# Converting the first two weight chunks by halves, and moving attention products next to scores

## The chip, the core and the metric

The kernel runs on one core of one Trainium2 chip. Its time is the device time of one launch in microseconds (us); the median of three runs of the kernel before is 542.89 us (542.35 to 542.96). TensorE (PE) multiplies matrices, VectorE (DVE), ScalarE (ACT) and GpSimd (POOL) work element by element, and SyncE (SP) issues most transfers. Each engine takes its own instructions in the order in which they stand in its queue.

## The reference

Inputs: `q`, `k`, `v` of shape (2, 8, 768, 64), weights of three layers, and two numbers, 8 global and 96 local positions. All arithmetic is float32.

```python
scores = q @ k.T / sqrt(64) - slope[h] * dist      # dist: to the key, or n_local for a global key
scores = where(keep, scores, -1e9)                  # keep: the 8 global keys, or the last 96 positions
a = exp(scores - max); a /= sum(a) + 1e-9
x = (a @ v) as (1536 tokens, 512)
h = x @ w_in                                        # 512 -> 2048
g = where(h > 0, h, exp(min(h, 0)) - 1)
x = g @ w_out                                       # 2048 -> 512
h = max(x @ w1, x @ w2, x @ w3)                     # 512 -> 768, three times
out = h @ w_out2                                    # 768 -> 512
```

## The kernel before, in words

Tokens are worked on in six groups of 256 (`GRP`), and three blocks of 512 (`BLOCKS`) for the first feed-forward layer. Attention is cut into 48 steps; step k is one tile of 128 queries for two heads. A step has these parts, each a method of `Windowed`: scores on PE (`scores_pe`, L214), a fused add and minimum on DVE (`scores_dve`, L239), exponentials with their sums on ACT (`scores_act`, `sums`), a reciprocal and a scaling on DVE (`recip`, `norm`), a transposition on PE (`turn_pe`, into a PSUM tile), its copy to SBUF (`turn_act`), and the product with the values on PE (`values_pe`, L318; `pair_pe` for two steps, `due_pe` for those that are due). The result is then copied (`pair_out`, `due_out`) or split at once into a high and a low part (`values_high`, `values_low`).

Steps 0 to 15 (the first block's tokens) run alone, in the loop of `windowed` at L1221. Steps 16 and 17 stand written out at L1250 to L1284, and steps 18 to 47 are laid beside the feed-forward layer in `Feed.run` (L765): one step to each column chunk `fc` (16 of them) of a block `bi`. For a chunk, `run` issues the product `h` of x with the chunk's `w_in` (12 matmuls, L674), then ELU on ACT and DVE (`elu_exp`, `elu_max`), the split of its result (`high` on ACT, `low` on DVE), and, one chunk late, the product `y` with the chunk's `w_out` (8 matmuls L705 and 4 matmuls L713). The same step's attention parts stand between these.

Weights come as 64-bit words and are converted on the chip before their first use, in the first block alone: a chunk is 128 x 2 x 512 (half 0 is `w_in`, half 1 `w_out`), and goes through `c_rebase` (ACT, L457), `c_low` (DVE, L461), two `c_word` (DVE, L468), `c_high` (ACT, L476) and `c_rest` (DVE, L481). Every one of these takes both halves in one instruction of 128 x 1024. In the loop of steps 0 to 15, a list of pieces, `words`, adds one piece of the conversion of chunks 0 and 1 to each step from step 8 (`CONV`) on. Chunk fc+1 is finished, and chunk fc+2 begun, beside chunk fc of the first block.

`FILL` (L43) adds two matmuls to the listed steps whose result nobody reads. The first four y tiles of a block are PSUM tiles that the block before has used; `save` (L721) copies them out first, half of it on ACT and half on DVE.

The order of the work is the order in which the code issues it; there is no scheduler.

## Time and profile before

| | |
|---|---|
| time of the runs, median | 542.89 us |
| the profiled execution's own time | 542.19 us |
| its span, first to last instruction | 540.4 us |
| PE busy | 530.7 us (98%) |
| DVE busy | 393.7 us (73%) |
| ACT busy | 288.0 us (53%) |
| chain that ended last | PE 91%, DVE 5%, ACT 3% |
| granted clock of PE, mean | 0.998 |

A span is the time from the first to the last instruction; the 1.8 us between it and the execution's time lie around it. Busy times of PE count each matmul to its modelled end, so neighbours overlap; what one matmul costs in a stream is the distance from its start to the next one's start. The busy shares are means over the whole span, and the stages differ: DVE is busy 90% or more in each fortieth of the span from 40.5 to 135 us, and 40% to 60% in most of those from 149 to 257 us. The rows that the prediction uses stand in a section of their own below.

### The profile page before, as it was taken

Reading aid. Unit: us, or ns where it says so; the run is one execution under the profiler, and the core shown is the slowest. Engines: PE = TensorE matmul, PEld = TensorE weight load, DVE = VectorE, ACT = ScalarE, POOL = GpSimd, SP = SyncE. Lnnn points to the kernel's source line nnn. Section 1 sums busy time; section 2 is a strip of 40 time slices with the busy share of each in tenths; the row PEclk is TensorE's granted clock in tenths of the full one; section 3 lists DMA queues with packets and bytes.
Section 4 is the critical chain, followed back from the end, with each engine's and each line's share of the span. In section 5 each row is a group of like instructions: output and inputs, shape, how many; then the busy total and the mean of one; then the engine's idle time right before and its main releaser. Section 6 shows DMA issues by size and latency. Waiting matters only on the chain.

```text
span 540.4 us, 7751 instructions
## 1 busy us (share of the span) xinstructions
PE 530.7 (98%) x2746; PEld 426.8 (79%) x2746; DVE 393.7 (73%) x828; ACT 288.0 (53%) x649; POOL 82.9 (15%) x89
## 2 busy tenths in 40 slices
PE   8999999999999999999999999999999999999995
PEld 6667787777777888888888888888888888888884
DVE  6889999999854444443567656787886989779883
ACT  5979877888845555554545655552157321224020
POOL 4220000000000000000000044321034410335000
PEclk9999999999999999999999999999999999999999
DMA  8929055442310111000000031331029301876014
GB/s 284 397 95 409 21 196 196 156 161 83 101 46 24 45 44 44 21 19 1 0 2 0 1 117 40 116 115 42 1 71 308 146 1 40 270 293 234 1 73 168
DMA packets 23455, 59.21 MB, mean 110 GB/s; under 512 B 2416, under 2 KB 2416, under 8 KB 23408
## 3 DMA queue, kind: packets, MB, share of 16 engines
q1 hardware_dynamic: 18368, 49.46, 26.5%
q10 hardware_dynamic: 5040, 9.18, 4.5%
q8 instruction: 24, 0.39, 0.3%
q14 instruction: 23, 0.19, 0.1%
HBM read 49.19 MB, written 9.44 MB: 108 GB/s over the span
## 4 chain that ended last, share of the span: by engine, by line
PE 91%; DVE 5%; ACT 3%; issue 0%; POOL 0%; ACTq 0%; POOLq 0%
PE h L674 26%; PE y L705 16%; PE y L713 8%; PE y L975 8%; PE y L1069 5%; PE y L674 5%; PE S L975 4%; PE TX L327 3%; PE TX L304 3%; PE S L228 3%; PE S L1069 2%; PE TX L975 2%; PE S L674 2%; PE h L975 2%; PE TX L1069 2%; ACT p L275 1%
## 5 line engine op out<-in xcount | busy, mean ns | idle before, releaser
L674 PE MATMUL h<-xh,w 128*128 128x512 f32 (+1 forms) x432 | 122.2, 387 | 0.2 <-ACT w L476 0.2
L705 PE MATMUL y<-gh,w 128*128 128x512 f32 x384 | 98.7, 399 | 0.1
L510 POOL TENSOR_TENSOR w<-wr,w 128x512 fp32r<-128x512 f32 x42 | 62.9, 1507 | 231.8 <-ACT w L509 220.5
L674 PEld LDWEIGHTS h<-xh,w 128*128 128x128 f32 x432 | 80.2, 188 | 17.9 <-ACT w L476 0.8
L705 PEld LDWEIGHTS y<-gh,w 128*128 128x128 f32 x384 | 69.7, 188 | 14.3 <-issue 0.5
L674 PE MATMUL h<-xl,w 128*128 128x512 f32 (+1 forms) x216 | 71.0, 386 | 0.0
L699 DVE SCALAR_TENSOR_TENSOR e<-e,h 128x512 f32<-128x512 f32 x48 | 32.9, 685 | 49.5 <-ACT e L695 49.4
L509 ACT CAST w<-wr 128x512 fp32r<-128x512 f32 x42 | 27.6, 663 | 63.4 <-DVE wr L500 51.1
L694 ACT ACTIVATE e<-h 128x512 f32<-128x512 f32 x48 | 28.7, 599 | 55.3 <-PE h L674 51.2
L275 ACT ACTIVATE p<-p,m 128x232 f32<-128x232 f32 (+1 forms) x96 | 44.9, 471 | 17.1 <-DVE m L254 16.9
L713 PE MATMUL y<-gl,w 128*128 128x512 f32 x192 | 51.6, 390 | 0.0
L500 DVE SCALAR_TENSOR_TENSOR wr<-wr 128x512 uint32<-128x512 uint32 x48 | 44.2, 921 | 7.5 <-ACT wr L492 6.0
L686 DVE TENSOR_TENSOR gl<-e,gh 128x512 fp32r<-128x512 f32 x48 | 33.1, 689 | 19.9 <-ACT gh L681 19.9
L674 PEld LDWEIGHTS h<-xl,w 128*128 128x128 f32 x216 | 40.4, 188 | 8.1 <-issue 0.2
L198 POOL TENSOR_SCALAR raw<-raw,qsc 128x256 f32<-128x256 f32 x24 | 16.8, 699 | 193.4 <-DMA raw<-qk 193.4
L975 PE MATMUL y<-t,w 128*128 128x512 f32 x180 | 42.7, 389 | 0.0
L713 PEld LDWEIGHTS y<-gl,w 128*128 128x128 f32 x192 | 36.0, 188 | 8.0 <-issue 0.3
L681 ACT CAST gh<-e 128x512 fp32r<-128x512 f32 x48 | 29.6, 616 | 23.5 <-DVE e L699 23.3
L468 DVE SCALAR_TENSOR_TENSOR wr<-wr 128x1024 uint32<-128x1024 uint32 (+1 forms) x36 | 39.8, 1120 | 0.4
L975 PEld LDWEIGHTS y<-t,w 128*128 128x128 f32 x180 | 33.8, 188 | 7.0
L695 ACT ACTIVATE e<-e 128x512 f32<-128x512 f32 x48 | 30.3, 632 | 1.5
L985 ACT CAST g<-m 128x512 fp32r<-128x512 f32 x18 | 10.9, 621 | 35.2 <-DVE m L1004 27.0
(155 smaller groups left out, 837.5 us busy)
## 6 DMA issues: line engine op xcount, KB each, us to landing
wr<-wa SPq DMA_DIRECT2D x14, 1024.0 KB, 6.9
wr<-wb SPq DMA_DIRECT2D x24, 512.0 KB, 4.6
v<-v SPq DMA_DIRECT2D x24, 256.0 KB, 2.8
part<-row ACTq DMA_DIRECT2D x24, 256.0 KB, 4.6
raw<-qk SPq DMA_DIRECT2D x16, 312.0 KB, 4.6
row<-part SPq DMA_DIRECT2D x12, 256.0 KB, 3.1
out<-rows ACTq DMA_DIRECT2D x11, 256.0 KB, 2.3
raw<-qk SPq DMA_DIRECT2D x8, 260.0 KB, 4.7
```

The source lines that it names most:

```text
L275: self.nc.scalar.activation(p[:, o], p[:, o], AF.Exp, bias=m[:, u:u + 1], scale=-1.0, accum_out=m[:, 2 + u:3 + u],)
L468: self.nc.vector.scalar_tensor_tensor(r[..., 0], r[..., 1], v, r[..., 0], op0=op, op1=ALU.bitwise_or)
L500: self.nc.vector.scalar_tensor_tensor(t, a, c, t, op0=op, op1=ALU.bitwise_or)
L510: nc.gpsimd.tensor_tensor(w[:, u, 1], v, w[:, u, 0].bitcast(F32), op=ALU.subtract)
L674: nc.tensor.matmul(out[:, o:n], w[:, part % 2, c * P:c * P + P], (xl if part == 2 else xh)[:, c, o:n], start=(c, part) == order[0], stop=( ...
L686: (engine or self.nc.vector).tensor_tensor(gl[:, 0:n], e[:, 0:n], gh[:, 0:n].bitcast(F32), op=ALU.subtract)
L695: self.nc.scalar.activation(e, e, AF.Exp, scale=-1.0)
L699: self.nc.vector.scalar_tensor_tensor(e, e, -1.0, h, op0=ALU.add, op1=ALU.max)
L705: self.nc.tensor.matmul(y[e][:, 0:n], w[:, a, e * P:e * P + P], g[0][:, 0:n], start=fc == 0 and a == 0, stop=False,)
L713: self.nc.tensor.matmul(y[e][:, 0:n], w[:, 0, e * P:e * P + P], g[1][:, 0:n], start=False, stop=fc == NFC - 1,)
L975: self.nc.tensor.matmul(out, w[:, u, i % 2, b + c * P:b + c * P + P], o[:, i // 2, c], start=c == i == 0, stop=c == 1 and i == 2,)
L1069: nc.tensor.matmul(o, t[:, a, r], w[:, u, b], start=u == k == 0, stop=u == 1 and k == 2,)
```

## The change

Chunks 0 and 1 are converted by halves (the methods take `h`), half 0 in the loop of steps 8 to 15, half 1 later. Steps 18 and 19, with the chunks fc = 0 and 1 of the first block, leave `run` and stand in a new method, `begin`, in an order of their own; `run` starts at fc = 2 there. The filling matmuls of steps 8 to 13 go. At the first two chunks of the second block (steps 34 and 35) the value products are now those that are due (`joint = bi < 2`), and stand ahead of the scores.

```diff
-FILL = {1: 2, 2: 2, 8: 2, 9: 2, 10: 2, 11: 2, 12: 2, 13: 2}
+FILL = {1: 2, 2: 2}
...
-    def parts(self, c):
+    def parts(self, c, h=None):
+        hs = slice(0, 2) if h is None else slice(h, h + 1)
         if c in self.whole:
-            return [(self.whole[c], slice(0, 2))]
+            return [(self.whole[c][:, hs], hs)]
...
+    def begin(self, at, k, x, h):
+        copy, n = self.nc.scalar.copy, BLOCKS[0]
+        w = self.w[1][:, 0]
+        at.load_values(k)
+        self.w_ahead(4)
+        at.scores_pe(k, m=2)
+        at.turn_pe(k - 2, "y2")
+        h1 = self.ps.tile([P, 512], F32, tag="y3", name="h1")
+        self.product(h1, w, x, n, 0, 0, 4, BEHIND)
+        at.recip(k - 1)
+        at.norm(k - 1)
+        self.c_low(1, 1)
+        at.turn_pe(k - 1)
+        self.product(h1, w, x, n, 0, 4, 8, BEHIND)
+        e = self.elu_exp(h, n)
+        at.turn_act(k - 2, copy)
+        at.turn_act(k - 1, copy)
+        self.elu_max(e, h)
+        at.scores_dve(k)
+        gh = self.high(e, n)
+        gl = self.low(e, gh, n)
+        prev = gh, gl
+        self.c_high(0, 1)
+        self.c_rebase(2)
+        self.c_low(2)
+        self.c_rest(0, 1)
+        self.c_word(2, 0)
+        at.pair_pe(k - 2)
+        e = self.elu_exp(h1, n)
+        self.elu_max(e, h1)
+        at.scores_act(k)
+        at.sums(k)
+        at.pair_out(k - 2, copy)
+        y = self.out_tiles()
+        self.out_high(y, 0, prev, n)
+        self.out_low(y, 0, prev, n)
+        self.c_word(2, 1)
+        at.recip(k)
+        at.norm(k)
+        self.c_high(2)
+        k += 1
+        at.turn_pe(k - 1)
+        at.turn_act(k - 1, copy)
...
+        self.c_rest(2)
+        at.scores_dve(k)
+        at.scores_act(k)
+        at.sums(k)
+        gh = self.high(e, n)
+        self.c_word(1, 0, 1)
+        self.c_word(1, 1, 1)
+        self.c_high(1, 1)
+        self.c_rebase(3)
+        at.recip(k)
+        at.norm(k)
+        gl = self.low(e, gh, n)
+        self.c_rest(1, 1)
+        self.c_low(3)
+        self.c_word(3, 0)
+        return y, (gh, gl)
...
-                joint = fc > 1
+                joint = bi < 2
...
+                late = bi == 0 or fc > 0
+                if not late:
+                    at.due_out(due, nc.vector.tensor_copy)
+                    if joint:
+                        at.turn_pe(k - 1)
                 if left:
                     self.out_low(*left)
-                late = bi == 0 or fc > 0
                 if not late:
                     at.turn_act(k - 1, nc.vector.tensor_copy)
-                    if k % 2 == 0:
-                        at.pair_pe(k - 2)
                     at.scores_dve(k)
                     e = self.elu_exp(h, n)
                     at.scores_act(k)
-                    if k % 2 == 0:
-                        at.pair_out(k - 2, nc.scalar.copy)
...
         def convert():
-            f.c_rebase(0)
-            f.c_low(0)
+            f.c_rebase(0, 0)
+            f.c_low(0, 0)
             yield
-            f.c_word(0, 0)
-            f.c_rebase(1)
+            f.c_word(0, 0, 0)
+            f.c_rebase(1, 0)
             yield
-            f.c_word(0, 1)
+            f.c_word(0, 1, 0)
+            f.c_low(1, 0)
             yield
-            f.c_high(0)
-            f.c_low(1)
+            f.c_high(0, 0)
+            f.c_word(1, 0, 0)
             yield
-            f.c_rest(0)
+            f.c_rest(0, 0)
+            f.c_rebase(0, 1)
             yield
-            f.c_word(1, 0)
+            f.c_word(1, 1, 0)
+            yield
+            f.c_high(1, 0)
+            f.c_low(0, 1)
+            yield
+            f.c_rest(1, 0)
             yield
...
         at.values_low(k - 4, x)
+        f.c_word(0, 0, 1)
         at.scores_pe(k, m=2)
...
         at.values_high(k - 2, x)
+        f.c_rebase(1, 1)
         at.scores_act(k)
         at.scores_dve(k + 1, True)
         at.values_low(k - 2, x)
+        f.c_word(0, 1, 1)
         at.values_pe(k - 1)
...
-        f.run(at, first + 2, x, h, lambda: covered(nc, at.const, ni, flag))
+        begun = f.begin(at, k + 2, x, h)
+        f.run(at, first + 4, x, begun, lambda: covered(nc, at.const, ni, flag))
```

DVE, from the reciprocal of step 17 on, before: `wr_283` is chunk 1 as loaded, `wr_401` chunk 2, `w_712` chunk 1 converted, `m` the sums of a step, `p` its probabilities, `e` the ELU.

```order
L266 RECIPROCAL m_651<-m_651 128x2
L288 TENSOR_SCALAR p_650<-p_650,m_651 128x232 x2
L468 SCALAR_TENSOR_TENSOR wr_283<-wr_283 128x1024
L699 SCALAR_TENSOR_TENSOR e_702<-e_702,h_145 128x512
L254 ISA p_708,m_709<-S0_695,rel_105 128x232
L254 ISA m_709 128x1
L254 ISA p_708,m_709<-S1_696,rel_105 128x232
L254 ISA m_709 128x1
L461 TENSOR_SCALAR wr_401<-wr_401 128x1024
L481 TENSOR_TENSOR w_712<-wr_283,w_712 128x2x512
L266 RECIPROCAL m_709<-m_709 128x2
L288 TENSOR_SCALAR p_708<-p_708,m_709 128x232 x2
```

DVE behind the scores of step 18 (`p_716`) in the changed kernel: `wr_395` is now chunk 2, `w_456` and `w_766` are chunks 0 and 2 converted, `h1_688` is the product of fc = 1, and `p_778` belongs to step 19.

```order
L689 TENSOR_TENSOR gl_722<-e_710,gh_720 128x512
L462 TENSOR_SCALAR wr_395<-wr_395 128x1024
L482 TENSOR_TENSOR w_456<-wr_205,w_456 128x512
L469 SCALAR_TENSOR_TENSOR wr_395<-wr_395 128x1024
L702 SCALAR_TENSOR_TENSOR e_737<-e_737,h1_688 128x512
L469 SCALAR_TENSOR_TENSOR wr_395<-wr_395 128x1024
L266 RECIPROCAL m_717<-m_717 128x2
L288 TENSOR_SCALAR p_716<-p_716,m_717 128x232 x2
L482 TENSOR_TENSOR w_766<-wr_395,w_766 128x2x512
L254 ISA p_778,m_779<-S0_677,rel_105 128x232
L254 ISA m_779 128x1
L254 ISA p_778,m_779<-S1_678,rel_105 128x232
```

Chunk 1 is whole ahead of chunk 2's words before; now its second half comes behind the scores of step 19, and the low part of chunk 2 stands ahead of those scores.

PE behind the first product of the second block, before: `p_1659` and `p_1712` are steps 32 and 33, `S0_1790` and `S1_1791` the scores of steps 34 and 35, `y` the last chunk of the first block.

```order
L304 MATMUL TX_1785<-ident_126,p_1712 116x128 x4
L228 MATMUL S0_1790<-raw_1604 128x232
L228 MATMUL S1_1791<-raw_1604 128x232
L228 MATMUL S0_1790<-raw_1604 128x232
L228 MATMUL S1_1791<-raw_1604 128x232
L713 MATMUL y_787<-gl_1733,w_1663 128x512
L713 MATMUL y_788<-gl_1733,w_1663 128x512
L713 MATMUL y_789<-gl_1733,w_1663 128x512
L713 MATMUL y_790<-gl_1733,w_1663 128x512
L327 MATMUL TX_1785<-p_1659,v_1633 64x128 x4
L327 MATMUL TX_1785<-p_1712,v_1633 64x128 x4
```

The same place now: `p_1653` is step 32 and `p_1706` step 33.

```order
L327 MATMUL TX_1779<-p_1653,v_1627 64x128 x4
L228 MATMUL S0_1784<-raw_1598 128x232
L228 MATMUL S1_1785<-raw_1598 128x232
L228 MATMUL S0_1784<-raw_1598 128x232
L228 MATMUL S1_1785<-raw_1598 128x232
L304 MATMUL TX_1792<-ident_126,p_1706 116x128 x4
L716 MATMUL y_746<-gl_1727,w_1657 128x512
L716 MATMUL y_747<-gl_1727,w_1657 128x512
L716 MATMUL y_748<-gl_1727,w_1657 128x512
L716 MATMUL y_749<-gl_1727,w_1657 128x512
```

The transposition of step 33 has moved from ahead of the scores to behind them, the value product of step 32 to the head, and that of step 33 to the next even step.

## Rows read from the trace of the kernel before

**Rows 1.** Busy time by stretch: PE, PEld, DVE, ACT, POOL; clock; DMA share, GB/s

```profile
13.50:27.00 13.50, 12.89 (x111) 8.71 (x111) 12.09 (x53) 12.82 (x48) 3.10 (x5) 1.00 1.03 396
```

**Rows 2.** Chain of waits, attention's end: start us, us, what

```profile
51.93 1.13 ACT w L476
```

**Rows 3.** PE's timeline, first block: start us, us, instruction, count, idle before and releaser

```profile
53.10 0.50 PE L674 MATMUL h<-xh,w 128*128 128x512 f32 x1 [0.21 <-ACT w L476]
...
57.71 0.65 PE L304 MATMUL TX<-ident,p 128*116 128x128 f32 x4
...
66.87 0.40 PE L674 MATMUL h<-xh,w 128*128 128x512 f32 x1
```

**Rows 4.** DVE's timeline, steps 8 to 23

```profile
18.18 0.40 DVE L254 CUSTOM_DVE_ANT_0 p<-S,rel 128x232 f32<-128x232 f32 x1 [0.34 <-PE S L228]
...
20.55 0.39 DVE L254 CUSTOM_DVE_ANT_0 p<-y,rel 128x232 f32<-128x232 f32 x1
...
22.09 1.22 DVE L468 SCALAR_TENSOR_TENSOR wr<-wr 128x1024 uint32<-128x1024 uint32 x1
...
39.38 0.40 DVE L254 CUSTOM_DVE_ANT_0 p<-S,rel 128x232 f32<-128x232 f32 x1 [0.69 <-PE S L228]
...
43.25 0.17 DVE L266 RECIPROCAL m<-m 128x2 f32<-128x2 f32 x1 [0.29 <-ACT m L237]
...
52.36 0.39 DVE L254 CUSTOM_DVE_ANT_0 p<-S,rel 128x232 f32<-128x232 f32 x1
...
56.07 2.48 DVE L468 SCALAR_TENSOR_TENSOR wr<-wr 128x1024 uint32<-128x1024 uint32 x2
...
79.21 0.69 DVE L699 SCALAR_TENSOR_TENSOR e<-e,h 128x512 f32<-128x512 f32 x1 [0.44 <-ACT e L695]
```

**Rows 5.** DVE's timeline: conversion of late chunks, which comes by halves already

```profile
134.82 0.76 DVE L461 TENSOR_SCALAR wr<-wr 128x512 uint32<-128x512 uint32 x2
...
138.00 2.49 DVE L468 SCALAR_TENSOR_TENSOR wr<-wr 128x512 uint32<-128x512 uint32 x4
```

**Rows 6.** ACT's timeline, first block

```profile
40.73 0.49 ACT L275 ACTIVATE p<-p,m 128x232 f32<-128x232 f32 x1
...
52.96 0.49 ACT L275 ACTIVATE p<-p,m 128x232 f32<-128x232 f32 x1
...
56.24 0.60 ACT L694 ACTIVATE e<-h 128x512 f32<-128x512 f32 x1 [0.41 <-PE h L674]
...
57.41 0.25 ACT L390 COPY xraw<-TX 128x128 f32<-128x128 f32 x1
...
65.50 1.13 ACT L476 CAST w<-wr 128x1024 fp32r<-128x1024 f32 x1
```

**Rows 7.** PE's timeline, start of the second block

```profile
154.27 0.60 PE L304 MATMUL TX<-ident,p 128*116 128x128 f32 x4
154.80 1.05 PE L228 MATMUL S<-raw 64*128 64x232 f32 x8
...
156.90 1.09 PE L327 MATMUL TX<-p,v 116*64 116x128 f32 x16
...
161.16 2.08 PE L705 MATMUL y<-gh,w 128*128 128x512 f32 x8
```

**Rows 8.** DVE's timeline there

```profile
154.91 0.69 DVE L315 COPY p<-TX 116x512 f32<-116x512 f32 x1 [1.96 <-PE TX L304]
...
159.07 0.17 DVE L266 RECIPROCAL m<-m 128x2 f32<-128x2 f32 x1 [1.86 <-ACT m L237]
159.27 0.59 DVE L288 TENSOR_SCALAR p<-p,m 128x232 f32<-128x232 f32 x2
159.78 1.41 DVE L727 COPY yraw<-y 128x256 f32<-128x256 f32 x4
```

**Rows 9.** ACT's timeline there

```profile
158.04 0.37 ACT L363 COPY xraw<-TX 128x256 f32<-128x256 f32 x1 [0.66 <-PE TX L327]
```

**Rows 10.** Busy time by stretch, 2 us of steps 6 to 8

```profile
16.00:18.00 2.00, 1.43 (x12) 0.91 (x12) 1.81 (x10) 1.47 (x7) 0.00 (x0) 1.00 1.05 388
```

57 lines of the change are left out of this document (26 added, 31 removed).

## The prediction

> **What bounds the kernel now.** I read the stretches first, then the chain of waits, then the timelines of PE, DVE and ACT around the places that the diff touches. PE is the bound over the span, but not in the attention stage. There, in 13.5 to 27 us, DVE is busy 12.09 and ACT 12.82 of 13.50 us [rows 1], and a step of attention follows the step before at the pace of DVE: its own part of a step takes 22.09 - 20.55 = 1.54 us, and the piece of weight conversion behind it up to 1.22 us more [rows 4]. PE waits inside each step. The chain runs through DVE, ACT and PE by turns until the conversion of chunk 2 (the high part, ACT, 51.93 us [rows 2]) releases the third product of the first block at 53.10 us [rows 3]. From there PE is nearly closed, with DVE close behind it: on DVE the first wait for a result that PE bounds comes at 79.21 us, 0.44 us long [rows 4]. The number to watch is therefore not when attention ends, but when the product of chunk 4 starts, 66.87 us [rows 3], since its weights are ready only about 0.3 us ahead of it: the high part starts at 65.50 and takes 1.13 us [rows 6]. What moves that start moves the end; what comes back before it does not.
>
> **The filling matmuls and the halves in steps 8 to 15.** The twelve fills go from an engine that waits in these steps anyway, so they are worth nothing by themselves; DVE's list hides them, and if DVE were faster by more than 0.5 us a step they would begin to count.
>
> On DVE six whole pieces leave steps 8 to 13, four at about 1.2 (2.48 for two [rows 4]) and two at about 0.7, as two halves of the same operation take 0.76 [rows 5]: 6.2 us. In their place come, by step 13, five halves at 2.49 / 4 = 0.62 and two at 0.38 [rows 5], 3.9 us, and 1.0 us more in steps 14 and 15. DVE enters step 8 at 18.18 us either way [rows 4]; with its 0.23 us of waiting there, 8 x 1.54, and 4.9 us of pieces it is through step 15 at 35.6; with one wait of about 0.3 us for PE, which has six matmuls of the product ahead of the scores of step 15, 35.9. Then follow a reciprocal, a scaling and a split (about 0.9 of the 1.54) and the moved half word (0.62): 37.4 us. PE, from the scores of step 15 at 33.5, does a transposition, values, six matmuls, a transposition, values and the scores of steps 16 and 17 (0.55 + 0.6 + 0.9 + 0.55 + 0.6 + 1.0): 37.7 us, and that comes last. Before, these scores start on DVE at 39.38, also after a wait for PE [rows 4]. Lead: 1.7 us.
>
> **The lead in `begin`.** ACT has a half rebase (about 0.55 us, half of a whole one, near the 1.13 of the high part [rows 2]) ahead of the exponentials of step 16, which start at 40.73 before [rows 6] and about 39.5 now: the lead is 1.2. DVE's reciprocal of step 17 moves with it, from 43.25 [rows 4] to 42.1. From there to the last word of chunk 2, at 51.8, DVE had 8.5 us of work without a wait. Out of this piece go the word and the low part of chunk 1 (2.4 us) and the reciprocal and scaling of step 18, which now stand behind it (0.7). A half `c_low`, a half low part and a second `elu_max` come in (0.38 + 0.62 + 0.6), and two waits on ACT, about 0.15 for the ELU and 0.6 for its high part, which stands on ACT behind both copies of steps 16 and 17: 8.5 - 2.4 - 0.7 + 1.6 + 0.75 = 7.75. The last word is done at 49.85, chunk 2's high part starts at 49.9 in place of 51.93 [rows 2], and the third product at 51.05 in place of 53.10 [rows 3]. The lead has its largest value here, 2.05 us.
>
> Then it is given back. Before, DVE is at the scores of step 19 at 52.36 [rows 4], with the words of chunk 3 done at 56.07 + 2.48 = 58.5. Now it first has to wait for the high part of chunk 2 (51.0), take its low part (1.2), and only then the scores of step 19, at 52.15 to 52.2; behind these stand two half words and a half low part of chunk 1 (3 x 0.62) that were not there before, less the whole low part just paid (1.2), plus a wait of 0.25 for the sums: 58.5 - 0.2 + 1.9 - 1.2 + 0.25 gives 59.2. DVE is then 0.6 us behind the kernel before. ACT: the exponentials of step 19 start at 52.85, against 52.96; from there to the copy that frees the TX tile it took 57.41 - 52.96 - 0.41 of waiting = 4.04 us [rows 6], and now takes a half high part (0.57) more: 57.45. The transposition of step 19 on PE needs that copy: 57.7, against 57.71 [rows 3]. PE, which has the scores of steps 20 and 21 done at 55.3, waits there for some 2.4 us with the y matmuls of fc = 1 and the product of chunk 3 behind it, and the lead is gone. The words of chunk 4 follow 0.5 us late on DVE, its high part starts at 65.7 in place of 65.50 [rows 6], and the product of chunk 4 at 66.85, against 66.87. The 0.5 us on DVE vanish in the 0.44 us that it waits at 79.21 [rows 4]. **First block: 0.0 us.** Bounds: a gain of the whole 2.05, if the chunk-4 product comes as early as the third one; a loss of 1, if the lag on DVE is twice what I count.
>
> **Values next to scores.** The second block's first product is followed, before, by a transposition at 154.27, the scores, the old block's y matmuls, and the values of two steps at 156.90 [rows 7]. The values of step 33 (half of 1.09) go to a later step, so no work is saved. What moves is the transposition of step 33: it now stands behind one value product (about 0.6) and the scores (1.0), and starts at 154.27 + 1.7 = 156.0. Its copy on DVE moves from 154.91 [rows 8] to 156.65, and behind this copy stand, on DVE, the scores of step 34, `elu_max`, the reciprocal, the scaling, and the four copies that free the old y tiles. ACT loses the copy at 158.04, with its 0.66 of waiting [rows 9], which wins part of it back: exponentials from 157.95 to 158.9, high part of the ELU 0.5, sums 0.2, so the reciprocal starts at 159.65 in place of 159.07, and the copies at 160.35 in place of 159.78 [rows 8]. The first y tile is free after the third of four copies, 3/4 of 1.41 later: 161.45, against a start of 161.16 [rows 7]. PE, which is ready at 160.5, waits 0.9 us; it starts y 0.3 us later than before, and the postponed values (about 0.45 us more in the step of fc = 2) are still to do. **Second block: +0.7 us.** Bounds: -0.2, if the y tiles do not bind (160.5 in place of 161.16, and 0.45 postponed); +1.2 if the reorder costs its full shift of 1.7 less the 0.5 that PE does not do there.
>
> **Sum.** 542.19 us of the profiled execution (540.4 of span and 1.8 around it) + 0.0 + 0.7 = 542.9. The median of the runs is 542.89, 0.7 above the profiled one, so against the median the forecast is 543.6.
>
> **The rivals.** (a) The lead survives: DVE and ACT wait less in `begin` than I count, and the product of chunk 4 starts up to 2 us earlier. For it: three waits of 0.15 to 0.6 us that I only worked out stand in the piece, and PE would be ready for chunk 4's product without the wait of 2.4 us. Against it: DVE's list to that point has the same work, somewhat more by halves, and had only short waits before (0.69, 0.29 [rows 4]). It gives 543.6 - 2.0 = 541.6; with the second block free as well, 540.9.
>
> (b) Slower: the lag of the conversion on DVE. It decides from the 0.3 us by which the weights of chunk 4 are ahead of their product; each microsecond of lag beyond goes into the time. If the halves and their waits cost 1.5 us and not 0.6, the product of chunk 4 starts 1.1 us late: 543.6 + 1.1 = 544.7.
>
> (c) The clock. Without fills PE idles more in steps 8 to 15. Steps 3 to 7 have none already, and in 16 to 18 us PE is busy 1.43 of 2.00 us with the clock granted in full, 1.00, which is the level of 2.4 GHz [rows 10]; steps 8 to 15 will be busier than that. At the level of 1.2 GHz the 1.43 would be 2.86, 0.86 more per 2 us, or 0 to 7 us over the eight steps; I take 3, 546.6. The Trainium skill, "TensorE: Matmul & The Clock Gate", section "What's actually happening", has the half rate as the default, which activity lifts; by this rule the missing fills speak against the change. The trace of the stretch without fills does not show the fall.
>
> **How the numbers follow.** What a measurement of this kernel can tell from no change is about 0.2%, 1.1 us: 541.8 to 544.0. The forecast, 543.6, has a chance of 0.50 with its own spread of about 0.6 us, so most of it is "same" and some "slower". (a) 0.32, of which four fifths are below 541.8; (b) 0.13, nearly all slower; (c) 0.05. Faster 0.27, same 0.51, slower 0.22. The range of 8 in 10 reaches from 540.9, the full gain of (a), to 545.0, just past (b).
>
> **What would show it.** In the changed kernel's profile: scores of step 16 on DVE near 37.7 us; the third product near 51.05; a PE wait of about 2 us ahead of the transposition of step 19, which starts near 57.7; the chunk-4 product at 66.9; at the second block, the four y copies on DVE about 6.1 us behind the start of the transposition's old place, counted from the end of the block's first product (5.5 before), and a PE wait ahead of the first y matmul. I am wrong if the chunk-4 product starts before 66, if PE does not wait at the second block's first y matmul, or if the granted clock falls below 1.00 between 18 and 36 us.

## The result and the profile after

The changed kernel takes 545.73 us (median of 6 runs, 545.34 to 546.23), the kernel before 542.91 on the same chip (6 runs, 542.35 to 544.01): a ratio of 1.0051, with an interval of 1.0039 to 1.0063. That is 2.8 us slower, and 0.7 above the upper end of the range. The profiled execution took 546.23 us, its span is 544.3, at a mean granted clock of 0.999.

For the rest I count from one event, VectorE's scores of step 8, at 18.18 us before and 18.75 after. Up to there both kernels do the same; the 0.57 us come from the start, most of them from a load that landed 0.4 us later in this one execution. "Product of chunk c" is the first matmul of the h product of fc = c, "step 36" the scores of that step on TensorE. (The recorded expectations call the product that starts at 94.55 us before "fc=7". It is that of fc = 8.) In the changed kernel the code of these parts stands one to three lines further down: L674 is now L677, L699 is L702.

```
us from the scores of step 8          before   after   difference
scores of step 16, VectorE             21.20    19.76    -1.44
product of chunk 2                     34.92    33.79    -1.13
scores of step 19, VectorE             34.18    34.91    +0.73
transposition of step 19               39.53    40.22    +0.69
product of chunk 3                     42.76    43.60    +0.84
product of chunk 4                     48.69    50.16    +1.47
product of fc = 8                      76.37    77.95    +1.58
step 36 (second block, fc = 2)        149.29   151.94    +2.65
```

So there is a lead of 1.4 us, it is lost and becomes a lag of 1.5 between the products of chunks 2 and 4; the lag changes by 0.1 up to the second block, and the start of the second block adds 1.07. Behind step 36 both kernels run the same distance, 365.9 us, to the last group of matmuls. From VectorE's last instruction to the end of the span, with the last store in it, it takes 5.5 us before and 6.1 in the changed kernel; over the profiles of all runs this varies from 5.4 to 6.1.

VectorE's timeline of the changed kernel, first block (as [rows 4]: start, us, instruction, in brackets the idle time ahead of it and what ended it):

```profile
38.51 0.40 DVE L254 CUSTOM_DVE_ANT_0 p<-S,rel 128x232 f32<-128x232 f32 x1
...
46.49 0.69 DVE L689 TENSOR_TENSOR gl<-e,gh 128x512 fp32r<-128x512 f32 x1 [1.08 <-ACT gh L684]
...
52.52 1.23 DVE L482 TENSOR_TENSOR w<-wr,w 128x1024 fp32r<-128x1024 f32 x1 [0.56 <-ACT w L477]
53.66 0.39 DVE L254 CUSTOM_DVE_ANT_0 p<-S,rel 128x232 f32<-128x232 f32 x1
...
54.30 1.57 DVE L469 SCALAR_TENSOR_TENSOR wr<-wr 128x512 uint32<-128x512 uint32 x2
55.79 0.15 DVE L266 RECIPROCAL m<-m 128x2 f32<-128x2 f32 x1
...
58.48 2.49 DVE L469 SCALAR_TENSOR_TENSOR wr<-wr 128x1024 uint32<-128x1024 uint32 x2
...
61.52 0.68 DVE L702 SCALAR_TENSOR_TENSOR e<-e,h 128x512 f32<-128x512 f32 x1
```

Before, VectorE had no wait between 43.25 and the words of chunk 3 at 56.07 [rows 4]. Now it waits 1.08 us for `gh` and 0.56 for the high part of chunk 2. ScalarE's timeline shows why, and what follows (as [rows 6]):

```profile
45.36 0.59 ACT L315 COPY p<-TX 116x512 f32<-116x512 f32 x1 [0.78 <-PE TX L304]
45.84 0.62 ACT L684 CAST gh<-e 128x512 fp32r<-128x512 f32 x1
...
58.66 0.25 ACT L390 COPY xraw<-TX 128x128 f32<-128x128 f32 x1
61.05 1.13 ACT L477 CAST w<-wr 128x1024 fp32r<-128x1024 f32 x1 [2.13 <-issue]
```

`gh` stands behind the turned copy of step 17, which waits for TensorE; `e` had been ready since about 44.8 (VectorE's maximum started at 44.09 and takes 0.69). The bracket of the last row names "issue", but VectorE ends the words of chunk 3 at 60.97, and the high part starts at 61.05: that is the release. TensorE's timeline (as [rows 3]):

```profile
52.54 0.50 PE L677 MATMUL h<-xh,w 128*128 128x512 f32 x1
...
58.97 0.65 PE L304 MATMUL TX<-ident,p 128*116 128x128 f32 x4 [1.85 <-ACT xraw L390]
...
62.35 0.47 PE L677 MATMUL h<-xh,w 128*128 128x512 f32 x1
...
68.91 0.50 PE L677 MATMUL h<-xh,w 128*128 128x512 f32 x1
```

The product of chunk 3 at 62.35 has three late suppliers: TensorE comes from the y matmuls that the transposition held up; the high part of chunk 3 ends at 61.05 + 1.13 = 62.18; and the ELU's maximum of fc = 2, which frees the PSUM tile `h`, ends at 61.52 + 0.68 = 62.20. The last two both stand behind the words of chunk 3 on VectorE. Which of them costs the time is not to be read from this; the runs below tell.

The start of the second block, TensorE and then VectorE (as [rows 7, 8]):

```profile
156.53 0.66 PE L327 MATMUL TX<-p,v 116*64 116x128 f32 x8
157.12 1.05 PE L228 MATMUL S<-raw 64*128 64x232 f32 x8
158.10 0.65 PE L304 MATMUL TX<-ident,p 128*116 128x128 f32 x4
158.50 1.17 PE L716 MATMUL y<-gl,w 128*128 128x512 f32 x4
160.77 1.66 PE L677 MATMUL h<-xh,w 128*128 128x512 f32 x6 [1.10 <-DVE e L702]
...
164.00 2.10 PE L708 MATMUL y<-gh,w 128*128 128x512 f32 x8
```

```profile
158.79 0.69 DVE L315 COPY p<-TX 116x512 f32<-116x512 f32 x1 [1.26 <-PE TX L304]
...
160.03 0.68 DVE L702 SCALAR_TENSOR_TENSOR e<-e,h 128x512 f32<-128x512 f32 x1
...
162.24 1.41 DVE L730 COPY yraw<-y 128x256 f32<-128x256 f32 x4
```

TensorE waits 1.10 us, but ahead of the product of fc = 1, not ahead of the y matmuls. Both products use the one PSUM tile `h`; the ELU's maximum frees it, and that stands on VectorE behind the turned copy and the scores. Of the 1.07 us, 0.69 are there when this product starts (142.02 us from the scores of step 8, 139.75 before). The other 0.38 come by the scores of step 36, ahead of which TensorE now has the value products of two steps in place of one.

The stretch without fills, and the clock in it (as [rows 1, 10]: PE, PEld, DVE, ACT, POOL busy; granted clock; DMA share, GB/s):

```profile
13.50:27.00 13.50, 11.32 (x96) 6.80 (x96) 12.26 (x60) 12.43 (x51) 2.59 (x5) 1.00 1.03 397
16.00:18.00 2.00, 1.62 (x16) 0.91 (x12) 1.93 (x11) 1.47 (x8) 0.00 (x0) 1.00 1.05 386
```

TensorE is busy 1.57 us less than in [rows 1], and the clock stays at 1.00, the level of 2.4 GHz.

### The profile page after: what moved, and what is told of

Read it like the earlier page. It is cut to its first block, busy times and chain, and to the rows that moved or that the text cites. A ratio compares the mean times of both kernels' runs of the same rounds, so it can differ in the third digit from the quotient of the medians.

```text
span 544.3 us, 7723 instructions
## 1 busy us (share of the span) xinstructions
PE 529.4 (97%) x2722; PEld 423.8 (78%) x2722; DVE 395.3 (73%) x837; ACT 288.0 (53%) x652; POOL 80.9 (15%) x89
## 4 chain that ended last, share of the span: by engine, by line
PE 88%; DVE 7%; ACT 3%; issue 1%; DMA 1%; SPq 0%; DVEq 0%; ACTq 0%
PE h L677 25%; PE y L708 15%; PE y L1036 7%; PE y L716 7%; PE y L1130 4%; PE y L677 4%; PE S L1036 4%; PE TX L327 3%; PE TX L304 3%; PE S L228 2%; PE S L1130 2%; PE TX L1036 2%; PE S L677 2%; PE h L1036 2%; DVE wr L469 2%; PE TX L1130 1%
## 5 line engine op out<-in xcount | busy, mean ns | idle before, releaser
L677 PE MATMUL h<-xh,w 128*128 128x512 f32 (+1 forms) x432 | 122.4, 388 | 1.3 <-DVE e L702 1.1
L677 PEld LDWEIGHTS h<-xh,w 128*128 128x128 f32 x432 | 80.2, 188 | 19.4 <-DVE e L702 1.5
L677 PE MATMUL h<-xl,w 128*128 128x512 f32 (+1 forms) x216 | 71.1, 386 | 0.0
L702 DVE SCALAR_TENSOR_TENSOR e<-e,h 128x512 f32<-128x512 f32 x48 | 32.9, 685 | 49.8 <-ACT e L698 49.6
L275 ACT ACTIVATE p<-p,m 128x232 f32<-128x232 f32 (+1 forms) x96 | 44.8, 469 | 19.8 <-DVE m L254 19.8
L677 PEld LDWEIGHTS h<-xl,w 128*128 128x128 f32 x216 | 40.4, 188 | 8.1 <-issue 0.2
L198 POOL TENSOR_SCALAR raw<-raw,qsc 128x256 f32<-128x256 f32 x24 | 14.8, 616 | 198.4 <-DMA raw<-qk 198.4
```

Of the source, the lines that this page charges most:

```text
L275: self.nc.scalar.activation(p[:, o], p[:, o], AF.Exp, bias=m[:, u:u + 1], scale=-1.0, accum_out=m[:, 2 + u:3 + u],)
L677: nc.tensor.matmul(out[:, o:n], w[:, part % 2, c * P:c * P + P], (xl if part == 2 else xh)[:, c, o:n], start=(c, part) == order[0], stop=( ...
L702: self.nc.vector.scalar_tensor_tensor(e, e, -1.0, h, op0=ALU.add, op1=ALU.max)
```

## The experiments

Fifteen kernels ran, up to four on one chip, each set beside its own runs of the kernel before. The last columns count as in the table above, each from one profiled execution; the same stretch of untouched code came out up to 0.2 us apart from one to the next (but for a fall of the clock, told below), so the columns are good to about that. The difference of two ratios is good to about 0.002, or 1 us, so the times alone do not tell most single moves apart; what a move is worth is read from the columns.

```
run              us, range               before   ratio, interval            chunk 4  fc = 8  fc = 8 to step 36
before                                                                        48.69    76.37     72.92
after            545.73 545.34-546.23    542.91   1.0051 [1.0039, 1.0063]     50.16    77.95     73.99
halves_only      544.19 543.68-544.61    543.16   1.0018 [1.0009, 1.0027]     49.70    77.36     72.89
whole_begin      546.12 546.00-546.24    543.16   1.0056 [1.0042, 1.0069]     51.01    78.80     73.95
old_block1       545.02 544.18-545.63    543.16   1.0031 [1.0021, 1.0042]     51.04    78.75     72.93
elu_first        545.39 544.85-545.57    543.16   1.0040 [1.0026, 1.0054]     50.97    78.58     73.73
due_sooner       545.47 545.12-546.28    543.22   1.0045 [1.0031, 1.0059]     50.21    78.00     74.00
rest_pool        549.91 549.48-550.26    543.22   1.0122 [1.0107, 1.0138]     51.04    79.90     76.59
pool_due         550.07 549.58-550.53    543.22   1.0128 [1.0113, 1.0144]     51.13    79.97     76.60
elu_save_first   545.33 544.69-546.27    543.22   1.0043 [1.0030, 1.0057]     50.01    77.79     73.71
gh_sooner        545.26 544.48-546.59    543.04   1.0050 [1.0036, 1.0063]     49.34    77.15     74.01
sums_first       544.09 543.67-545.08    543.04   1.0023 [1.0014, 1.0032]     50.11    77.90     72.61
first_fixed      543.03 542.59-543.93    543.04   1.0000 [0.9991, 1.0009]     49.00    76.75     72.97
all_fixed        542.77 542.28-543.31    543.04   0.9994 [0.9985, 1.0003]     48.99    76.77     72.53
block2_fixed     542.65 542.26-543.37    542.93   0.9995 [0.9986, 1.0004]     48.85    76.54     72.56
fills_gone       543.19 542.32-546.16    542.93   1.0010 [0.9997, 1.0023]     49.01    76.66     73.02
best             543.36 542.85-543.87    542.93   1.0006 [0.9997, 1.0015]     48.34    77.01     72.61
```

### The change taken apart

**halves_only**, on the kernel before:

```diff
     def parts(self, c):
         if c in self.whole:
-            return [(self.whole[c], slice(0, 2))]
+            r = self.whole[c]
+            if c in (0, 1):
+                return [(r[:, i:i + 1], slice(i, i + 1)) for i in range(2)]
+            return [(r, slice(0, 2))]
```

> The kernel before, with every piece of the conversion of chunks 0 and 1 as two instructions of half the size, in the same places. Theory H (a half costs more than half: 0.08 us more on DVE per pair of halves, and DVE's list sets when the product of chunk 4 starts): 12 more DVE instructions, DVE 0.7 to 1.2 us later at chunk 4, 0.3 of it hidden: 543.3 to 543.8. Rival O (only the new order of steps 18 and 19 costs): 542.9, the product of chunk 4 at 66.9 us of the trace.

Measured: 544.19, +1.0 us; the product of chunk 4 is 1.0 late. By VectorE's timeline the scores of step 16 are already 0.9 late (22.08 us from those of step 8, 21.20 before):

```profile
18.66 0.40 DVE L254 CUSTOM_DVE_ANT_0 p<-S,rel 128x232 f32<-128x232 f32 x1 [0.33 <-PE S L228]
...
19.73 0.82 DVE L288 TENSOR_SCALAR p<-p,m 128x232 f32<-128x232 f32 x2
...
40.74 0.40 DVE L254 CUSTOM_DVE_ANT_0 p<-S,rel 128x232 f32<-128x232 f32 x1 [0.69 <-PE S L228]
```

So cutting the pieces, in place, costs about 1 us by itself. In this profile the six pieces that VectorE has in steps 8 to 13 account for 0.4 of the 0.9 us: two half words take 1.21 us from their start to the next instruction's, a whole one 1.14. Nearly all the rest are two pairs of scalings, not cut, which took 0.82 us in place of 0.59 while a GpSimd multiplication ran (19.92 to 20.41 us beside the row above); whether the cutting brings such meetings about stays open. (The edit adds 8 VectorE instructions, not the 12 of the expectation.)

**whole_begin**, on the changed kernel: whole pieces, in the old places up to step 15; the last three of chunk 1 stand where the changed kernel has second halves, in steps 16 and 17; the written-out order of `begin` is kept.

```diff
         def convert():
-            f.c_rebase(0, 0)
-            f.c_low(0, 0)
+            f.c_rebase(0)
+            f.c_low(0)
 ...
     def begin(self, at, k, x, h):
 ...
-        self.c_word(1, 0, 1)
-        self.c_word(1, 1, 1)
-        self.c_high(1, 1)
 ...
-        f.c_word(0, 0, 1)
+        f.c_word(1, 1)
 ...
-        f.c_rebase(1, 1)
+        f.c_high(1)
 ...
-        f.c_word(0, 1, 1)
+        f.c_rest(1)
```

> The changed kernel with whole pieces again: chunks 0 and 1 are converted in the attention steps as before the change, the three pieces of chunk 1 that are left stand where the changed kernel has its second halves in step 16; the order of steps 18 and 19 is the changed one, without halves. Theory H: 1.2 us of DVE come back, the product of chunk 4 starts 0.9 to 1.2 us earlier than in the changed kernel: 544.5 to 544.8. Rival O: the waits of the order stay, 545.5 to 545.7.

Measured: 546.12, no better than the change, and the product of chunk 4 is 2.3 us late, 0.85 later than in the changed kernel. Theory H, which had it 0.9 to 1.2 sooner, did not come true. Cutting costs 1.0 in place and undoing it gains nothing, which points at the order of `begin`. The run does not separate the two cleanly, since the three whole pieces of chunk 1 also stand ahead of the product of chunk 2 here (35.64 us, 33.79 in the changed kernel); gh_sooner and first_fixed below test the order itself.

**old_block1**, on the changed kernel: the first group of the second block as before.

```diff
-                joint = bi < 2
+                joint = fc > 1
 ...
-                if not late:
-                    at.due_out(due, nc.vector.tensor_copy)
-                    if joint:
-                        at.turn_pe(k - 1)
 ...
+                    if k % 2 == 0:
+                        at.pair_pe(k - 2)
 ...
+                    if k % 2 == 0:
+                        at.pair_out(k - 2, nc.scalar.copy)
```

> The changed kernel with the start of the second block as it was before the change. Theory A (the new order there makes PE wait for the PSUM tile of the first product, which elu_max on DVE frees late): 1.1 us come back, 544.7, and the wait ahead of the block's second product (1.10 us in the changed kernel) is gone. Rival (the prediction's: only the copies of the y tiles come late): 0.7 back, 545.0, and the wait stays where it is. If the part costs nothing: 545.7.

Measured: 545.02, which is the rival's time; but the trace has theory A. From fc = 8 to step 36 it takes 72.93 us, as before: the second block's cost is gone, and with it TensorE's wait ahead of the block's second product. Beside its own runs of the kernel before it is 1.86 us slower, the changed kernel 2.82, so 0.96 of 1.07 are back. In its profiled execution (545.43) the clock fell in the first block. The stretches around TensorE's wait for the transposition of step 19 (columns as above, the granted clock behind POOL):

```profile
56.00:58.00 2.00, 0.72 (x8) 0.35 (x4) 1.97 (x4) 1.97 (x4) 0.00 (x0) 1.00 0.02 6
58.00:60.00 2.00, 1.43 (x8) 1.27 (x9) 1.89 (x2) 0.51 (x2) 0.00 (x0) 0.97 0.00 0
60.00:62.00 2.00, 2.00 (x6) 1.56 (x5) 2.00 (x7) 1.36 (x2) 0.00 (x0) 0.50 0.00 0
62.00:64.00 2.00, 2.00 (x7) 1.60 (x7) 1.96 (x5) 1.97 (x7) 0.00 (x0) 0.68 0.00 0
```

0.50 is the level of 1.2 GHz. The eight y matmuls at 58.97 us took 3.00 us, in the changed kernel 2.08. In this run and in elu_first (0.50 there too from 60 to 62 us) the product of chunk 4 is 0.8 us later than in the changed kernel. The mean granted clock is on record for every execution: 0.996 or more in each of the 81 runs of the kernel before that stand beside the experiments, and 0.994 or 0.995 in three of the eight of this run, one of six of the changed kernel, one of five of elu_first and two of five of elu_save_first. The two fastest of this run, 544.18 and 544.31, have 0.999. Where the clock fell in the executions without a profile is not recorded.

**elu_first**, on the changed kernel: the ELU's maximum ahead, in the second block's first group.

```diff
-                    at.turn_act(k - 1, nc.vector.tensor_copy)
-                    at.scores_dve(k)
                     e = self.elu_exp(h, n)
+                    self.elu_max(e, h)
+                    at.turn_act(k - 1, nc.vector.tensor_copy)
+                    at.scores_dve(k)
                     at.scores_act(k)
 ...
-                if not sooner:
+                if not sooner and late:
                     self.elu_max(e, h)
```

> The changed kernel; at the first group of the second block DVE does elu_max before the copy of the transposed probabilities and the scores, so the product's PSUM tile is free earlier. Theory A: the wait of 1.10 us ahead of the second product goes; the copies of the y tiles, which come late as well, then bind and PE waits some 0.6 us ahead of the first y matmul: 545.2 to 545.4. Rival (the tile does not matter, only DVE's amount of work): the second product starts as late as before, 545.7. Rival (nothing binds behind it): 544.6.

Measured: 545.39, theory A. The wait of 1.10 us is gone, and the y matmuls wait in its place:

```profile
159.70 1.52 PE L677 MATMUL h<-xh,w 128*128 128x512 f32 x6
...
163.65 2.08 PE L708 MATMUL y<-gh,w 128*128 128x512 f32 x8 [0.62 <-DVE yraw L730]
```

### What holds the first block

**due_sooner**, on the changed kernel:

```diff
+                    first = bi == 0 and fc == 2
+                    if first:
+                        at.due_out(due, nc.scalar.copy)
                     e = self.elu_exp(h, n)
                     if joint:
-                        at.due_out(due, nc.scalar.copy)
+                        if not first:
+                            at.due_out(due, nc.scalar.copy)
```

> The changed kernel with one move: in the group of fc=2 of the first block, the copy of the due values (ACT, L390) stands ahead of the ELU's two exponentials, not behind them. Theory W (the loss of the first block is TensorE's wait of 1.85 us at the transposition of step 19, which that copy releases): the transposition starts about 1.2 us sooner (39.0 us behind the scores of step 8, not 40.2), the products of chunks 3 and 4 follow 1.2 sooner, and the time is about 544.6 us. Theory D (VectorE's list is the loss, TensorE's wait only its shadow): the transposition moves by the same 1.2, but the product of chunk 3 needs that chunk's high parts, which ACT starts only when VectorE ends the words of chunk 3 at 60.97; the product moves by 0.1 at most, chunk 4's too, and the time stays at 545.4 to 545.9.

Measured: 545.47, theory D. The transposition comes 1.1 us sooner (57.53 - 18.40 = 39.13 us) and the product of chunk 3 does not move (43.66, 43.60 in the changed kernel); TensorE now waits there, for the ELU's maximum (it ends at 61.91), and the high part of chunk 3 ends at the same time (61.88):

```profile
57.53 0.65 PE L304 MATMUL TX<-ident,p 128*116 128x128 f32 x4 [0.70 <-ACT xraw L390]
...
62.06 0.47 PE L677 MATMUL h<-xh,w 128*128 128x512 f32 x1 [1.13 <-DVE e L702]
```

The wait of 1.85 us at the transposition, the largest that the profile of the changed kernel shows on TensorE in this block, was worth nothing here.

**rest_pool** and **pool_due**, on the changed kernel (pool_due has the edit of due_sooner as well): the remainder of the second half of chunk 1 and of every later whole chunk goes to GpSimd.

```diff
-            self.nc.vector.tensor_tensor(
-                w[:, hs, 1], r[..., 0].bitcast(F32), w[:, hs, 0].bitcast(F32), op=ALU.subtract
-            )
+            if h is None and c in self.whole:
+                todo = (self.nc.vector, slice(0, 1)), (self.nc.gpsimd, slice(1, 2))
+            else:
+                todo = ((self.nc.gpsimd if (c, h) == (1, 1) else self.nc.vector, hs),)
+            for eng, q in todo:
+                rr = r[:, q] if len(todo) > 1 else r
+                eng.tensor_tensor(
+                    w[:, q, 1], rr[..., 0].bitcast(F32), w[:, q, 0].bitcast(F32), op=ALU.subtract
+                )
```

> The changed kernel with the remainder w - high(w) of the second half (the half that the y products read) of chunk 1 and of every later whole chunk on GpSimd instead of VectorE. It takes 0.68 us (chunk 1) and 0.55 us (chunk 2) from VectorE's list ahead of the words of chunk 3, and about 0.55 us of each later step. Theory D (VectorE's list): the high parts of chunk 3 start 1.0 to 1.7 us sooner; but the copy that releases the transposition of step 19 is unmoved but for what the exponentials of step 19 gain (0.5), so the product of chunk 3 is 0.4 sooner, that of chunk 4 (50.16 us behind the scores of step 8) 0.5 to 1.0 sooner, and the time about 545.0 us. Theory W (TensorE's wait for the copy): nothing but the 0.5 moves, time 545.2. Against both stands that a subtraction of 128x512 takes 1.5 us on GpSimd and may slow VectorE beside it: then 545.7 or more.

> Both edits of the two runs beside it in the changed kernel: the copy of the due values ahead of the exponentials in the group of fc=2, and the remainders of the second halves on GpSimd. If the loss of the first block is two limits that end at the same time (VectorE's words of chunk 3, and TensorE's wait for the copy), this alone gives back what neither gives by itself: product of chunk 3 at 42.4 to 42.8 us behind the scores of step 8 (43.60 in the changed kernel, 42.76 before), that of chunk 4 at 48.7 to 49.0, and the time about 544.2 us, with the 1.07 us of the second block still in it. If either limit alone is the cause, this equals the better one of the two runs beside it.

Measured: 549.91 and 550.07. The objection in the expectation was right, and its lower bound of 545.7 is passed by 4 us. VectorE's timeline and GpSimd's in rest_pool:

```profile
56.74 1.79 DVE L462 TENSOR_SCALAR wr<-wr 128x1024 uint32<-128x1024 uint32 x1
...
62.88 1.81 DVE L488 TENSOR_TENSOR w<-wr,w 128x512 fp32r<-128x512 f32 x1
```

```profile
56.30 1.68 POOL L488 TENSOR_TENSOR w<-wr,w 128x512 fp32r<-128x512 f32 x1 [2.05 <-ACT w L477]
62.40 1.73 POOL L488 TENSOR_TENSOR w<-wr,w 128x512 fp32r<-128x512 f32 x1 [4.43 <-ACT w L477]
```

The low part at 56.74 takes 1.79 us (0.69 without GpSimd beside it), and the remainder at 62.88 1.81 (0.68). Both end 0.55 us behind GpSimd's instruction, so they did their work after it and not beside it. The Trainium skill, "SBUF — State Buffer", section "SBUF: two separate sides", has this as a rule for VectorE instructions in a two-port mode or with two inputs in SBUF: the port that the two engines share is locked for a whole instruction, and the other waits for all of it. The trace agrees here. These two runs say nothing on theories D and W.

**gh_sooner**, on the changed kernel:

```diff
         at.turn_act(k - 2, copy)
-        at.turn_act(k - 1, copy)
         self.elu_max(e, h)
+        gh = self.high(e, n)
+        at.turn_act(k - 1, copy)
         at.scores_dve(k)
-        gh = self.high(e, n)
         gl = self.low(e, gh, n)
```

> The changed kernel with one move on ACT in the group of fc=0: the high part of the ELU's output (gh) stands ahead of the turned copy of step 17 instead of behind it, so it no longer queues behind that copy's wait of 0.78 us for TensorE. Theory D (VectorE's list with its waits sets the first block): VectorE's wait of 1.08 us before gl goes, everything behind it on VectorE comes 1.0 us sooner (scores of step 19 at 33.9 us behind those of step 8, 34.9 in the changed kernel), the products of chunks 3 and 4 come 0.8 to 1.0 sooner (43.60 and 50.16 in the changed kernel), and the time is about 544.5 us. The rival (VectorE then waits 1.0 longer at the next thing that ACT or TensorE delivers, the high parts of chunk 2 or the product of fc=1): the products of chunks 3 and 4 move by under 0.3 and the time is 545.2 to 545.8.

Measured: by the profile theory D. VectorE takes `gl` without a wait, the scores of step 19 come at 34.2 us (34.91 in the changed kernel), and the products of chunk 4 and of fc = 8 are both 0.8 sooner:

```profile
45.04 0.69 DVE L689 TENSOR_TENSOR gl<-e,gh 128x512 fp32r<-128x512 f32 x1
...
51.42 1.23 DVE L482 TENSOR_TENSOR w<-wr,w 128x1024 fp32r<-128x1024 f32 x1 [0.55 <-ACT w L477]
52.56 0.40 DVE L254 CUSTOM_DVE_ANT_0 p<-S,rel 128x232 f32<-128x232 f32 x1
```

The five times (544.48 to 546.59, the profiled one the lowest) have a median of 545.26, which is not the 544.5 expected: 2.22 us over its runs of the kernel before, the changed kernel 2.82. TensorE's wait at the transposition is still 1.75 us long here. The two slowest, 545.38 and 546.59, have a mean granted clock of 0.996, the others 0.998 and 0.999, which would fit a fall of the clock there but does not show it.

**first_fixed**, on the changed kernel: gh_sooner, due_sooner, old_block1, and

```diff
-        self.c_rest(2)
         at.scores_dve(k)
         at.scores_act(k)
+        self.c_rest(2)
         at.sums(k)
```

> The changed kernel with the second block's first group as before, and three moves in the first block: gh of fc=0 ahead of the turned copy of step 17, the remainder of chunk 2 behind the scores of step 19 on VectorE (it waited 0.56 us there for the high parts), and the copy of the due values ahead of the ELU's exponentials in the group of fc=2. Halved chunks and the written-out order stay. Theory D, with no further wait behind these: the product of chunk 4 comes 1.2 to 1.5 us sooner (48.7 to 49.0 behind the scores of step 8, 50.16 in the changed kernel, 48.69 before), the second block costs nothing, and the time is 542.9 to 543.4 us, the same as before: the pieces' cost of 1.0 us and the order's gain then cancel. The rival (the order's waits move on): product of chunk 4 at 49.7 or later, time 544.5 or more.

Measured: 543.03, a ratio of 1.0000; the product of chunk 4 at 49.00, as expected. With three moves that take no work away, the first block's loss goes from 1.58 to 0.38 us at fc = 8. So most of the loss was the order's waits; without them the changed order makes up for most of the 1.0 us that the halves cost in place.

### What holds the second block

**elu_save_first**, on the changed kernel: elu_first, and

```diff
+                if left:
+                    ysave[bi - 1] = self.save(left[0], left[3])
                 if not late:
                     at.sums(k)
                     at.recip(k)
                     at.norm(k)
-                if left:
-                    ysave[bi - 1] = self.save(left[0], left[3])
```

> The changed kernel with two moves in the first group of the second block: the ELU's maximum ahead of the turned copy and the scores on VectorE (as in the run elu_first), and the copies of the y tiles ahead of the reciprocal and the two normalizations of the step. Theory A (two waits stand one behind the other, the h tile and then the copied y tiles): elu_first lost the wait of 1.10 us but got 0.62 us at the first y product; with the copies 0.75 us sooner that wait goes too, the distance from the product of fc=7 to the scores of step 36 falls by 0.8 to 1.0 us against the changed kernel, and the time is about 544.8 us. Theory B (the group has more work on VectorE than the place gives, so the wait moves on to the turned values of the step): the cost of 0.8 us stays, in a wait at the transposition of that step, and the time is 545.4 to 545.7.

Measured: 545.33, theory B: 73.71 us from fc = 8 to step 36, as in elu_first. The wait moved a second time, to the transposition of step 34:

```profile
162.87 0.62 PE L304 MATMUL TX<-ident,p 128*116 128x128 f32 x4 [0.91 <-DVE p L288]
```

VectorE's row behind it shows what is late, the sums (ACT, L237), which now stand behind four copies of y tiles:

```profile
162.18 0.17 DVE L266 RECIPROCAL m<-m 128x2 f32<-128x2 f32 x1 [1.17 <-ACT m L237]
```

**sums_first**, on elu_save_first:

```diff
                     at.scores_act(k)
+                    at.sums(k)
 ...
                 if not late:
-                    at.sums(k)
                     at.recip(k)
```

> The run elu_save_first with one move on ACT in the second block's first group: the sums of step 34 stand right behind its exponentials, ahead of gh and of the copies of the y tiles. Theory B (the wait in this group goes from one thing to the next along one chain: scores, exponentials, sums, reciprocal, normalizations, transposition): VectorE's wait of 1.17 us for the sums and TensorE's of 0.91 us at the transposition of step 34 go, the distance from the product of fc=7 to the scores of step 36 (72.92 us before, 73.99 in the changed kernel, 73.71 in elu_save_first) falls to 72.9 to 73.1, and the time is about 544.5 us. If the wait only moves on again (to the y products or the next ELU), that distance stays over 73.4 and the time is 545.1 or more.

Measured: 544.09, and 72.61 us from fc = 8 to step 36, 0.3 under the kernel before. TensorE has no wait left in the group:

```profile
159.01 1.52 PE L677 MATMUL h<-xh,w 128*128 128x512 f32 x6
...
161.74 0.60 PE L304 MATMUL TX<-ident,p 128*116 128x128 f32 x4
162.09 2.10 PE L708 MATMUL y<-gh,w 128*128 128x512 f32 x8
```

One chain was late as a whole, with three places where it showed.

### Together, and what stays

**all_fixed**, on the changed kernel: first_fixed without old_block1, and sums_first.

> As first_fixed in the first block, and the second block's first group of the change kept with the moves of sums_first (the ELU's maximum, the copies of the y tiles and the sums sooner). If both theories hold: product of chunk 4 at 48.7 to 49.0 us behind the scores of step 8, 72.9 to 73.1 us from the product of fc=7 to the scores of step 36, time 542.9 to 543.5 us. If only the one of the first block holds: about 544.2; if neither, 545.0 to 545.6.

Measured: 542.77, ratio 0.9994 (0.9985 to 1.0003), which can't be told from no change. Step 36 is at 149.30 us, before at 149.29: +0.40 in the first block, -0.39 in the second. One wait is left in the first block:

```profile
61.16 0.47 PE L677 MATMUL h<-xh,w 128*128 128x512 f32 x1 [1.21 <-DVE e L702]
```

**block2_fixed**, on the kernel before: the change's part in the second block, with the moves of sums_first.

> The kernel before with the change's second-block part alone (values next to scores, the due copy and the transposition of step 33 ahead of the left-over y products), and with the three moves of sums_first in that group. If the new start is a gain once its chain is in order: from the product of fc=7 to the scores of step 36 it takes 72.5 us as in all_fixed (72.92 before), and the time is 0.4 us under before, 542.6 to 542.8. If it only breaks even (all_fixed's 72.53 came from the first block's state): 543.0 to 543.3, no difference. If the new start is a loss: 543.7 or more.

Measured: 542.65, 0.28 under its runs of before, and 72.56 us from fc = 8 to step 36. By the profile a gain of 0.36, as in all_fixed; by the times (ratio 0.9995, 0.9986 to 1.0004) still within what the interval leaves open.

**fills_gone**, on the kernel before:

```diff
-FILL = {1: 2, 2: 2, 8: 2, 9: 2, 10: 2, 11: 2, 12: 2, 13: 2}
+FILL = {1: 2, 2: 2}
```

> The kernel before without the fills of steps 8 to 13, as the change has it, and nothing else. If the fills carry nothing (the forecast's own term): granted clock 1.00 in every stretch from 13.5 to 60 us, time within 0.2% of before. If they hold the clock (its rival c): a stretch between 16 and 40 us at a granted clock under 0.9 and a time of 545 us or more.

Measured: 543.19, ratio 1.0010 (0.9997 to 1.0023). In the profiled execution (542.91) the granted clock is 1.00 in each of seven stretches from 13.5 to 62 us, and the products of chunk 4 and of fc = 8 come 0.3 us later than before. So the fills carry next to nothing there. But two of the eleven times are high: 546.16, with a mean granted clock of 0.990, the lowest of all runs on record, and 545.12, with 0.996. The first is 3.0 us over the median, the size that rival (c) gave to a fall of the clock. No profile of them exists, so whether and where the clock fell in steps 8 to 15 is not known, and whether missing fills cost time in some executions stays open.

**best**, on all_fixed: chunks 3 and 4 by halves as well, with the half that the h product reads first converted first, and the ELU's maximum of fc = 2 ahead of the scores of step 20.

```diff
-                    self.c_word(fc + 1, 1)
+                    self.c_word(fc + 1, 1, 0 if fc in (2, 3) else None)
 ...
-                sooner = bi == 0 and k % 2
+                hh = bi == 0 and fc in (2, 3)
+                sooner = bi == 0 and (k % 2 or hh)
 ...
-                    self.c_high(fc + 1)
+                    self.c_high(fc + 1, 0 if hh else None)
+                    if hh:
+                        self.c_word(fc + 1, 0, 1)
+                        self.c_word(fc + 1, 1, 1)
 ...
```

> all_fixed with chunks 3 and 4 also by halves in the first block: the half that the h product reads first gets its words and its high part before the other half, and the ELU's maximum of fc=2 stands ahead of the scores of step 20, so that neither the h tile nor the high parts hold the product of chunk 3 (both ended together, 1.21 us after TensorE was free). If these two were all that held it: chunk 3's product starts at 41.2 to 41.6 us behind the scores of step 8 (42.43 in all_fixed, 42.76 before), that of chunk 4 at 47.8 to 48.3 (48.99 and 48.69), the lead stays to the end of the block, and the time is 541.4 to 542.2 us, under before. If VectorE's list as a whole is the limit (the lead is lost again by chunk 5 or 6, or the further pieces, some 0.3 us, add to it): product of chunk 4 at 48.9 or later and the time 542.6 to 543.2.

Measured: 543.36. The product of chunk 3 comes at 40.81 us (42.43 in all_fixed), that of chunk 4 at 48.34, and at fc = 8 it is 77.01, later than all_fixed's 76.77. TensorE's waits say where the lead went:

```profile
61.86 1.20 PE L677 MATMUL h<-xh,w 128*128 128x512 f32 x4 [0.79 <-DVE w L482]
63.40 0.65 PE L304 MATMUL TX<-ident,p 128*116 128x128 f32 x4 [0.34 <-ACT p L315]
...
69.02 1.20 PE L677 MATMUL h<-xh,w 128*128 128x512 f32 x4 [0.41 <-DVE w L482]
...
72.53 0.65 PE L304 MATMUL TX<-ident,p 128*116 128x128 f32 x4 [0.31 <-ACT xraw L390]
```

VectorE's remainders come late inside the products. VectorE's timeline shows no wait from 48 to 93 us here, so its own list is the limit, and more pieces make it longer. That is the expectation's second branch, though its numbers (chunk 4 at 48.9 or later, 542.6 to 543.2) did not come out either. No version beat the kernel before by more than a measurement can tell.

## Why the prediction was wrong

**"First block: 0.0 us"** is the step that failed: it measured +1.47 at the product of chunk 4 and +1.58 at fc = 8. Its parts, with 0.57 us taken off the times of the changed kernel:

- The lead in attention: predicted 1.7, the scores of step 16 at 37.7 us; measured 1.4, at 37.94. Nearly right, and TensorE came last there as forecast, if narrowly: its scores start at 37.42 and take 1.05 us, to 38.47, and VectorE's half word ends at 38.42.
- The third product: predicted 51.05, a lead of 2.05; measured 51.97, a lead of 1.1. The wait for `gh`, which I had at 0.6, is 1.08 long. I had seen that `gh` stands behind both copies, but not that the second of them itself waits 0.78 us for TensorE.
- The lag on VectorE behind it: predicted 0.6 at the end of chunk 3's words (59.2; by the sum's own numbers 59.25 and 0.75); measured 1.85 (60.40, against 58.55 before). This is the mis-sized term. Of the 1.15 us between 59.25 and 60.40, 0.24 are the smaller lead, 0.48 the longer wait for `gh`, and 0.25 the two half words of chunk 1, which took 1.49 us from their start to the next instruction's and not 1.24; the rest are pieces of 0.1 and less, among them the wait for chunk 2's high part (0.56; 0.45 by the forecast's times). gh_sooner and first_fixed show what the waits are worth: without those on `gh` and on chunk 2's high part, and with the due copy moved, 1.2 of the 1.58 us are back.
- "The lead is gone" at the transposition of step 19, by TensorE's wait: the wait is there, 1.85 us, but it is not the cause. due_sooner took 1.1 us of it away and gained nothing, since the high part of chunk 3 and the ELU's maximum, both behind VectorE's words, end when the held-up y matmuls do.
- "The 0.5 us on DVE vanish in the 0.44 us that it waits at 79.21" came too late to help: the product of chunk 4 had started 1.47 late by then, and TensorE shows no wait behind it up to the second block that could have taken the lag up.
- The cost of cutting was sized about right: half a word takes 0.60 us from its start to the next instruction's (22.48 to 23.08), 0.62 in the sum. The 1.0 us of halves_only is that of a kernel that keeps both halves in the attention steps.

Rival (b) is what happened in the first block: it said that the lag decides from 0.3 us on, and that costs of 1.5 and not 0.6 would make chunk 4's product 1.1 late. The lag was 1.85 and the product 1.47 late. I gave it 0.13; the waits that would have moved that chance stand in the piece that I worked out by hand, without a row for them.

**"Second block: +0.7 us"** measured +1.07 (old_block1 takes all of it back). The chain was the right one (the later transposition of step 33, its copy on VectorE, and all that stands behind), the place was wrong. Counted from the block's first product, the transposition (4.4 us) and its copy (5.1) came where the forecast has them, and the y copies 0.3 sooner; yet the first y matmul came 0.7 later than before, not 0.3, and the postponed values added 0.4. I looked at the y copies; the ELU's maximum stands in the same list, ahead of them, and frees the tile of the next product, which TensorE needs first. The y copies were second in line (elu_first: 0.62), the sums third (elu_save_first: 0.91). Of the three signs of being wrong that the prediction set, this one came true: TensorE does not wait at the first y matmul. None of them stood for a late product of chunk 4.

**The fills at 0** held, as far as one profile and a ratio of 1.0010 go, with the two high times of fills_gone left open. **Rival (c)** had the clock fall in steps 8 to 15, where it stayed at 1.00. It did fall elsewhere, behind TensorE's wait at the transposition of step 19, in two of the profiled runs, though not in the profile of the changed kernel itself, so it is no part of the 2.65 us counted here. How much of the medians it carries is not known.

## What to carry to other kernels

When one wait is made to go by moving work, list for each engine everything that stands behind the moved instruction, and ask of every one which tile it frees and who needs that first; here six moves of an instruction or a small group, with no work taken away, brought back the whole loss of 2.8 us (ratio 1.0051 in the changed kernel, 0.9994 in all_fixed). A long wait on the engine that bounds the kernel is not yet its loss: take the releaser away and see whether the next instruction moves, since a second supplier can end at the same time. Cutting instructions in halves can help where the first half is waited for (in best, with the ELU's maximum moved as well, the product of chunk 3 came 1.6 us sooner), but it lengthens the list of its engine: the lead of best was gone by fc = 8, and halves_only, where the halves stay side by side, cost 1.0 us.
